# Another written order for the engines' work, fewer filler matmuls and another assignment of tiles to buffers

## The chip, the cores and the metric

The kernel runs on one core of one Trainium2 chip. The core has five engines with instruction sequences of their own: TensorE (PE: matrix products; PEld is its weight load), VectorE (DVE), ScalarE (ACT), GpSimd (POOL), and SyncE (SP), which here issues DMA transfers. Each engine takes its instructions in order. The metric is the device time of one execution in microseconds; several runs are taken, and their median and range are given.

## The reference

```python
# attention: B=4, H=8, S=768, D=64; inputs n_global (8) and n_local (96)
scores = q @ k.transpose(0, 1, 3, 2) / sqrt(D)
keep   = is_global | is_local        # the first 8 keys, and 0 <= i - j < 96
scores = scores - slope[head] * dist # dist: |i - j|, or 96 for a global key that isn't local
a      = softmax(where(keep, scores, -1e9))
x      = (a @ v), heads side by side # 3072 tokens x 512
# feed-forward
h   = x @ w_in                       # 512 -> 2048
g   = where(h >= 1, h, where(h <= -1, 0, (h + 1)**2 / 4))
out = g @ w_out                      # 2048 -> 512
```

The weights arrive as 64-bit floats, q and k as 32-bit floats in blocks of 128 tokens with the head dimension on the partitions.

## The kernel before

The 3072 tokens are 24 units of 128 tokens, numbered 0 to 23: first the four first blocks of the batches (units 0 to 3), then the other five blocks of each batch. Attention is done unit by unit, in two halves of four heads (hf 0 and 1). Two units make a chunk of 256 tokens; the feed-forward part runs over 12 chunks, 0 to 11. Numbers are held as pairs of 16-bit floats, a high part and the rest (names in h and l), so a product takes three matmuls.

**Units 0 to 3** use 32-bit data: first_load (L612) fetches k, q and v, first_scores (L620) makes the scores, masked (L632) adds the bias and takes the minimum on VectorE, expo (L644) the exponential on ScalarE, first_turn (L668) and first_pt (L675) transpose, first_av (L686), scale_x (L694) and first_xt finish the half unit. **Units 4 to 23**: fetch loads a block, conv_hi (L749, ScalarE) and conv_lo (L759 on VectorE for v, L764 and L765 on GpSimd for k and q) split it into halves, conv_check (L773) takes a square sum on ScalarE for a check of the numbers' size. keep_glob (L781, L784) saves the first 32 keys or values of the batch, and set_glob (L792, L794) puts them into a later block. Then scores (L810), masked, expo, split_p (L824 on ScalarE, L826 on VectorE), a transposing DMA, attend (L851), scale_x, split_x and another transposing DMA.

**Weights** come in 32 pieces (0 to 15 of w_in, 16 to 31 of w_out): w_load (L518) is a load of 512 KB on SyncE's queue, w_bits (L532, L536, L540) makes 32-bit floats of the 64-bit ones on VectorE, w_hi (L553, ScalarE), w_scale (L560) and w_lo (L567, GpSimd) split them.

**Feed-forward.** ffn1 (L936) multiplies a chunk by two weight pieces into an h tile; gelu works on it in steps (L955 on ScalarE, L959 and L961 on VectorE, then L969 to L985 on GpSimd and ScalarE) and writes ga and gb tiles. Chunks 0 to 2 multiply these plainly by w_out: ffn2 (L995). Chunks 3 to 11 use a scheme with fewer products: first_products and last_products (L1039) use differences of the weights that diff (L1008 to L1030) prepares once, and fold (L1090, L1093) puts the parts together. put_out stores the result on SyncE's queue.

limits (L429, L431) spreads the two input numbers over the partitions with a small matmul. filler is one 128x512 matmul of zeros (L494) into a tile called spare that nobody reads.

**The order.** Each step is a call that is put into a list called plan, sorted by a planned time. It isn't issued in that order: the list PLACE holds the numbers of the plan's entries, and the calls are made in its order. Each engine's sequence is so the part of PLACE that concerns this engine. An assertion, after(), makes sure that a step that needs another's result stands behind it. Entries 89 to 288 are the 200 fillers; PLACE need not name them all, and 69 are named before.

**The buffers.** Tiles have tags ("ga", "z", "s", ...), and each tag has a fixed number of buffers, two to thirteen. SLOTS says which of them the n-th tile of the tag takes. A tile's first writer waits until all users of the tile that held the buffer before are done.

```python
n = taken[tag] = taken.get(tag, -1) + 1
return p.tile(shape, dtype, tag=f"{tag}_{SLOTS[tag][n]}", bufs=1, name=name)
...
for n in PLACE or range(len(plan)):
    t, _, f, args = plan[n]
    f(*args)
```

Of the kernel before, what the change touches and what calls it, by code (L numbers as in the profile page):

```python
# [26 lines left out]
GLOB = 32  # L27
# [5 lines left out]
SV = 256.0  # L33
# [5 lines left out]
SQK = 128.0  # L39
# [19 lines left out]
HE = {"k": "p", "q": "p", "v": "v"}  # L59
# [282 lines left out]
def fast_path(ctx, tc, q, k, v, nraw, nval, w_in, w_out, out, half, one, stat, marks, badi):  # L342
# [392 lines left out]


    fetched, kblk, kglob, vblk, vglob, qblk = ({} for _ in range(6))

    def fetch(u, kind, j):
        b, i = UNITS[u]  # L740
        r = tl(ins, [P, DM], F32, "in", INS, f"{kind}r{u}_{j}")
# [738 lines left out]
```

## Time and profile before

| | |
|---|---|
| median of the runs | 602.26 us (601.92 to 602.86, 3 runs) |
| the profiled execution | 603.65 us; its span, from the first to the last instruction, 601.8 us |
| granted clock of TensorE, mean | 0.997 of full speed |
| busy over the span | TensorE 580.5 us (96%), GpSimd 500.2 (83%), VectorE 477.7 (79%), ScalarE 441.5 (73%) |
| DMA | 88.19 MB, mean 147 GB/s |

The profile is of one execution, which took a little longer than the runs that were timed. Busy shares are means over the whole span; the stages differ, and the stretch up to about 200 us, in which the first units, the weights and the first chunks are worked on, looks different from what follows.

### The profile page before, as it was taken

Reading aid. Unit: us, or ns where it says so; the run is one execution under the profiler, and the core shown is the slowest. Engines: PE = TensorE matmul, PEld = TensorE weight load, DVE = VectorE, ACT = ScalarE, POOL = GpSimd, SP = SyncE. Lnnn points to the kernel's source line nnn. Section 1 sums busy time; section 2 is a strip of 40 time slices with the busy share of each in tenths; the row PEclk is TensorE's granted clock in tenths of the full one; section 3 lists DMA queues with packets and bytes.
Section 4 is the critical chain, followed back from the end, with each engine's and each line's share of the span. In section 5 each row is a group of like instructions: output and inputs, shape, how many; then the busy total and the mean of one; then the engine's idle time right before and its main releaser. Section 6 shows DMA issues by size and latency. Waiting matters only on the chain.

```text
span 601.8 us, 16582 instructions
## 1 busy us (share of the span) xinstructions
PE 580.5 (96%) x6275; PEld 478.8 (80%) x6275; DVE 477.7 (79%) x1175; ACT 441.5 (73%) x1146; POOL 500.2 (83%) x570
## 2 busy tenths in 40 slices
PE   8999998799999999999999999999999999999995
PEld 4777764356777688888888889888888888898884
DVE  6999999889987667888888888879989878883331
ACT  4998997889866778858787778768768768634330
POOL 5368996695999998899998998899898799579880
PEclk9999999899999999999999999999999999999999
DMA  7647678479660266467598468388487576250011
GB/s 245 207 153 233 203 247 258 102 148 171 123 141 12 62 153 164 119 156 203 131 179 202 125 153 205 104 213 203 120 204 158 153 180 154 77 124 1 2 36 41
DMA packets 144236, 88.19 MB, mean 147 GB/s; under 512 B 108180, under 2 KB 124820, under 8 KB 144148
## 3 DMA queue, kind: packets, MB, share of 16 engines
q1 hardware_dynamic: 144144, 87.05, 57.4%
q8 instruction: 51, 0.84, 0.6%
q14 instruction: 37, 0.30, 0.2%
q10 hardware_dynamic: 4, 0.00, 0.0%
HBM read 54.53 MB, written 6.29 MB: 101 GB/s over the span
## 4 chain that ended last, share of the span: by engine, by line
PE 75%; POOL 9%; DVE 7%; ACT 4%; issue 2%; DMA 2%; POOLq 0%; DVEq 0%; ACTq 0%
PE h L936 31%; PE o L1039 28%; PE o L995 5%; PE av L851 4%; PE s L810 4%; POOL ga L969 2%; DMA wd<-in_moe_w_in_dram 2%; PE spare L494 1%; DVE wd L540 1%; POOL wd L1030 1%; DVE w_bits L532 1%; DVE u L961 1%; POOL kh L765 1%; ACT z L644 1%; DVE w_bits L536 1%
## 5 line engine op out<-in xcount | busy, mean ns | idle before, releaser
L936 PE MATMUL h<-xt,wih 128*128 128x256 f16 x1536 | 255.7, 273 | 3.4 <-DVE u L961 3.4
L936 PE MATMUL h<-xt,wil 128*128 128x256 f16 x768 | 209.4, 273 | 0.0
L936 PEld LDWEIGHTS <-wih 128*128 128x128 f16 x1536 | 148.7, 98 | 27.1 <-DVE u L961 7.7
L644 ACT ACTIVATE z<-z,stat 128x256 f32<-128x256 f32 (+1 forms) x192 | 91.5, 479 | 14.6 <-DVE stat L632 14.6
L980 POOL TENSOR_TENSOR ga<-u,ga 128x512 f16<-128x512 f32 x72 | 89.8, 1249 | 11.2 <-ACT ga L978 10.8
L959 DVE SCALAR_TENSOR_TENSOR h<-h,u 128x512 f32<-128x512 f32 x96 | 66.3, 692 | 38.9 <-ACT u L955 38.4
L1039 PEld LDWEIGHTS <-ga 128*128 128x128 f16 x864 | 83.2, 98 | 10.1
L955 ACT ACTIVATE u<-h,half 128x512 f32<-128x512 f32 x96 | 65.0, 677 | 27.2 <-PE h L936 14.4
L936 PEld LDWEIGHTS <-wil 128*128 128x128 f16 x768 | 75.1, 98 | 8.7
L971 POOL TENSOR_TENSOR u<-u 128x256 f32<-128x256 f32 x72 | 59.9, 835 | 20.0 <-DVE u L961 19.0
L985 POOL TENSOR_TENSOR gb<-u,gb 128x384 f16<-128x384 f32 x72 | 70.2, 978 | 3.5 <-ACT gb L983 3.5
L1039 PE MATMUL o<-wd,ga 128*128 128x256 f16 x432 | 70.7, 273 | 0.0
L1039 PE MATMUL o<-woh,ga 128*128 128x256 f16 x288 | 70.7, 273 | 0.0
L1039 PEld LDWEIGHTS <-gb 128*128 128x128 f16 x648 | 62.4, 98 | 8.0 <-issue 0.6
L978 ACT ACTIVATE ga<-u 128x512 f16<-128x512 f32 x72 | 44.2, 621 | 32.9 <-POOL u L973 30.4
L961 DVE SCALAR_TENSOR_TENSOR u<-u,h 128x512 f32<-128x512 f32 x96 | 65.1, 679 | 3.3 <-POOL kg L781 0.5
L826 DVE SCALAR_TENSOR_TENSOR ph<-z,ph 128x1024 f16<-128x1024 f32 x40 | 56.8, 1423 | 13.0 <-ACT ph L824 13.0
L995 PE MATMUL o<-woh,ga 128*128 128x512 f16 x192 | 61.7, 384 | 1.4 <-ACT woh L553 0.8
L632 DVE CUSTOM_DVE_ANT_0 z<-s,bias 128x256 f32<-128x256 f32 x160 | 58.3, 414 | 5.7 <-PE s L810 5.5
L1039 PE MATMUL o<-wd,gb 128*128 128x256 f16 x432 | 60.4, 273 | 0.6 <-DVE ob L1090 0.6
L995 PEld LDWEIGHTS <-ga 128*128 128x128 f16 x288 | 27.7, 99 | 37.6 <-issue 9.4
L599 DVE TENSOR_REDUCE stat<-c_raw 128x1 f32<-128x256 f32 x128 | 47.9, 405 | 0.0
(132 smaller groups left out, 1185.3 us busy)
## 6 DMA issues: line engine op xcount, KB each, us to landing
wd<-in_moe_w_in_dram SPq DMA_DIRECT2D x16, 512.0 KB, 4.8
wd<-in_moe_w_out_dram SPq DMA_DIRECT2D x16, 512.0 KB, 4.4
c_raw<-in_moe_w_in_dram SPq DMA_DIRECT2D x32, 256.0 KB, 3.0
c_raw<-in_moe_w_out_dram SPq DMA_DIRECT2D x32, 256.0 KB, 3.3
kr<-in_k_dram SPq DMA_DIRECT2D x28, 256.0 KB, 4.1
vr<-in_v_dram SPq DMA_DIRECT2D x28, 256.0 KB, 3.2
qr<-in_q_dram SPq DMA_DIRECT2D x24, 256.0 KB, 4.3
out_dram<-ob SPq DMA_DIRECT2D x23, 256.0 KB, 2.7
```

Of the source, the lines that this page charges most:

```text
L632: nc.vector.tensor_tensor_reduce(out=p32[u, hf][:, hh, :], in0=pts[u, hf][hh // 2][:, hh % 2, 0:n], in1=(own_bias if n == P else bias)[:, ...
L644: nc.scalar.activation(z, z, AF.Exp, bias=nm[:, c : c + 1], scale=-1.0, accum_out=sums[:, c : c + 1])
L826: nc.vector.scalar_tensor_tensor(phs[u, hf][:, 1, :], zf, SP_, phs[u, hf][:, 0, :], op0=ALU.mult, op1=ALU.subtract)
L936: nc.tensor.matmul(hp[:, :, e, :], w[:, dc, f], xt[:, hf, 2 * a + j, :], start=(n == 0), stop=(n == 3 * NDC - 1),)
L955: nc.scalar.activation(u, h, AF.Relu, bias=half, scale=2.0 / (SV * SW), accum_out=su[:, col : col + 1])
L959: nc.vector.scalar_tensor_tensor(h, h, 4.0 / (SV * SW), u, op0=ALU.mult, op1=ALU.max)
L961: nc.vector.scalar_tensor_tensor(u, u, 4.0, h, op0=ALU.min, op1=ALU.mult)
L971: nc.gpsimd.tensor_sub(f[:, 3:7:3], f[:, 0:6:5], f[:, 4:5].to_broadcast([P, 2, P]))
L980: nc.gpsimd.tensor_sub(gas[c, g][:, 1], f[:, 0:4], gas[c, g][:, 0])
L985: nc.gpsimd.tensor_sub(gbs[c, g][:, 1, 0:3], f[:, 4:7], gbs[c, g][:, 0, 0:3])
L995: nc.tensor.matmul(po, a, w[:, f, :], start=(f == 0 and n == 0), stop=(f == NFC - 1 and n == 2))
L1039: nc.tensor.matmul(acc[:, e], x, w, start=first and n == 0, stop=last and n == 2)
```

## The change

Three things. The list PLACE is another permutation of the same entries, without the 32 fillers 126 to 157, so that 37 fillers remain. The digits of SLOTS are others, for all tags; "kg" (the saved global keys) uses one buffer where it used two. And an empty tuple VPU is added, with a function he() that would let some units' v be converted on GpSimd: with VPU empty, conv_lo, conv_check and keep_glob issue what they issued before.

```diff
 PLACE = [
-    1, 2, 0, 13, 41, 4, 28, 20, 10, 3, 46, 89, 90, 91, 92, 93, 5, 8, 6, 11, 7, 51, 19, 94, 95, 96, 97, 98, 99, 100,
-    21, 18, 56, 16, 31, 17, 64, 38, 34, 43, 39, 14, 69, 30, 15, 37, 29, 47, 9, 74, 26, 22, 33, 12, 24, 25, 88, 23, 32,
...
+    0, 2, 1, 10, 13, 8, 20, 11, 4, 29, 3, 5, 6, 7, 89, 90, 91, 31, 15, 21, 16, 19, 18, 14, 38, 30, 39, 43, 34, 41, 26,
+    47, 25, 9, 37, 17, 92, 93, 94, 45, 12, 36, 33, 23, 22, 32, 58, 61, 24, 55, 27, 49, 95, 96, 97, 68, 40, 54, 35, 67,
+    62, 65, 48, 66, 42, 44, 75, 57, 98, 52, 79, 83, 59, 87, 85, 28, 77, 71, 81, 301, 63, 84, 60, 73, 289, 304, 292,
...
 ]
 SLOTS = {
...
-    "k": [int(n, 16) for n in "012012012012102102102102"],
-    "kg": [int(n, 16) for n in "0101"],
-    "o": [int(n, 16) for n in "101010100101010101010101010101010101101010101"],
...
+    "k": [int(n, 16) for n in "201201021020120120120120"],
+    "kg": [int(n, 16) for n in "0000"],
+    "o": [int(n, 16) for n in "101001101010101001100101101001010110010110101"],
...
+VPU = ()
...
+    def he(kind, u):
+        return "p" if kind == "v" and u in VPU else HE[kind]
...
-        if HE[kind] == "v":
+        if he(kind, u) == "v":
...
-            nc.vector.tensor_copy(vglob[b], vblk[b, 0][0:GLOB])
+            (nc.gpsimd if u in VPU else nc.vector).tensor_copy(vglob[b], vblk[b, 0][0:GLOB])
```

The numbers in words, for four stretches of the list on which the prediction rests (each engine's own sequence, only the steps that count there; "fillers 5" is five of them in a row, the numbers of a step are unit and half, weight piece, or pair of pieces and step):

```
TensorE, start    before: positions, fillers 5, limits, fillers 7, first_scores 0.0 and 0.1, fillers 16, first_scores 1.0
                  after:  positions, limits, fillers 3, first_scores 0.1 and 0.0, fillers 3, first_scores 1.0
SyncE, start      before: q0, k0, q1, weight 2, v1, v0, k1, weights 0 and 1, q2, k2, weight 3
                  after:  k0, q0, k1, q1, weight 0, v0, weight 1, k2, q2, weights 2 and 3, v1
ScalarE, piece 31 before: conv_check 6, split_p 4.0, w_hi 31, expo, w_scale 31
                  after:  expo, split_p 4.0, w_hi 31, w_scale 31
VectorE, unit 7   before: set_glob 8, norm 6.0, conv_lo 7, diff 2.0, norm 6.1, diff 2.2, split_p 7.0
                  after:  diff 2.0, diff 2.2, norm 6.1, conv_lo 7, masked 7, split_p 7.0, diff 3.0
```

## Rows read from the trace of the kernel before

**Rows 1.** Busy us (and instructions) of each engine by stretch, granted clock, DMA share, GB/s.
```profile
0.00:50.00 50.00, 45.79 (x334) 32.67 (x334) 42.95 (x160) 39.72 (x124) 26.56 (x32) 1.00 0.62 201
50.00:117.00 67.00, 60.08 (x491) 41.06 (x492) 62.66 (x121) 58.97 (x132) 57.77 (x55) 0.99 0.65 206
117.00:200.00 83.00, 79.21 (x847) 55.30 (x847) 69.34 (x150) 63.45 (x161) 73.59 (x69) 0.98 0.64 130
200.00:588.00 388.00, 387.41 (x4539) 342.78 (x4534) 300.42 (x742) 279.40 (x731) 342.29 (x416) 1.00 0.57 137
```

**Rows 2.** Groups by line: the fillers (busy us, mean ns | idle before).
```profile
L494 PE MATMUL spare<-zeros 128*128 128x512 f16 x69 | 19.8, 409 | 0.0
```

**Rows 3.** Chain that ended last, 117 to 200 us: start us, us, what.
```profile
140.00 1.49 PE s L810 x48
...
144.55 0.58 DVE vh L759
145.13 0.61 DVE d L1008
...
146.27 1.65 POOL df L1023
...
186.58 2.79 PE h L936 x24
```

**Rows 4.** Timeline, TensorE at the start: start us, us, what.
```profile
2.91 2.31 PE L494 MATMUL spare<-zeros 128*128 128x512 f16 x5
...
9.05 3.63 PE L494 MATMUL spare<-zeros 128*128 128x512 f16 x16
12.61 0.71 PE L620 MATMUL s<-kr,qr 64*128 64x128 f32 x8
```

**Rows 5.** Timeline, VectorE; in brackets the idle time before and its releaser.
```profile
5.78 0.16 DVE L431 COPY nval<-pps_n 128x2 f32<-128x2 f32 x1 [0.38 <-PE pps_n L429]
...
9.16 0.29 DVE L632 CUSTOM_DVE_ANT_0 z<-s,wd 128x128 f32<-128x128 f32 x1 [0.92 <-PE s L620]
...
13.35 0.29 DVE L632 CUSTOM_DVE_ANT_0 z<-s,wd 128x128 f32<-128x128 f32 x1 [1.64 <-PE s L620]
...
21.31 0.70 DVE L532 TENSOR_SCALAR spare<-wd 128x512 int32<-128x512 int32 x1 [0.70 <-DMA wd<-in_moe_w_in_dram]
...
75.74 0.70 DVE L959 SCALAR_TENSOR_TENSOR h<-h,u 128x512 f32<-128x512 f32 x1 [1.01 <-ACT u L955]
...
112.71 1.22 DVE L826 SCALAR_TENSOR_TENSOR ph<-z,ph 128x1024 f16<-128x1024 f32 x1 [1.12 <-ACT ph L824]
```

**Rows 6.** Timeline, SyncE's DMA queue at the start.
```profile
2.12 0.43 SPq L518 DMA_DIRECT2D wd<-in_moe_w_in_dram  x1
...
3.62 0.43 SPq L612 DMA_DIRECT2D kr<-in_k_dram  x1
```

**Rows 7.** Timeline around the last weight piece.
```profile
109.86 0.69 DVE L540 SCALAR_TENSOR_TENSOR wd<-wd,w_bits 128x512 int32<-128x512 int32 x1
...
112.58 0.61 ACT L553 ACTIVATE woh<-wd 128x512 f16<-128x512 f32 x1
...
115.50 0.38 PE L995 MATMUL o<-wol,ga 128*128 128x512 f16 x1 [1.87 <-POOL wol L567]
...
115.71 0.59 PE L995 MATMUL o<-woh,ga 128*128 128x512 f16 x2
...
118.45 1.06 PE L995 MATMUL o<-woh,ga 128*128 128x512 f16 x2
```

**Rows 8.** Timeline of two places in the dense part.
```profile
380.11 0.52 ACT L983 ACTIVATE gb<-u 128x384 f16<-128x384 f32 x1 [0.90 <-POOL u L975]
...
381.37 0.49 PE L1039 MATMUL o<-wd,gb 128*128 128x256 f16 x3
...
416.43 1.37 POOL L980 TENSOR_TENSOR ga<-u,ga 128x512 f16<-128x512 f32 x1 [0.20 <-ACT ga L978]
...
417.69 0.49 PE L1039 MATMUL o<-wd,ga 128*128 128x256 f16 x3
```

More of the change, by code (lines that the diff above doesn't have):

```diff
@@ L107 @@
 PLACE = [
[159 rows of a table removed]
[158 rows of a table added]
 ]
 SLOTS = {
-    "ga": [int(n, 16) for n in "0123456789abc012589bc3467a012589bc3467058b360a129c475b809c57836a124b0958614057c3a2b98615a3b61407c2985ab10c95b364728a105b67215c9348a0b725930a261c48b75901247b03ac65891243"],
-    "h": [int(n, 16) for n in "01010101011010101010101010101010101010110010110010101010010101010101010101101010101010101010110011010101010"],
-    "in": [int(n, 16) for n in "01234501254301425304123542015320410231542310542013204532012531402351403251402351"],
-    "k": [int(n, 16) for n in "012012012012102102102102"],
@@ L273 @@
-    "kg": [int(n, 16) for n in "0101"],
-    "o": [int(n, 16) for n in "101010100101010101010101010101010101101010101"],
-    "ob": [int(n, 16) for n in "01220120102101201201201201201021"],
-    "ph": [int(n, 16) for n in "01010101010110101010101010101010101010101010"],
-    "pt": [int(n, 16) for n in "010101010101010110101010101010101010101010100101"],
-    "q": [int(n, 16) for n in "01010101100101010101"],
-    "r": [int(n, 16) for n in "010110101001010110010101010101101001010101011001"],
-    "raw": [int(n, 16) for n in "0101010101010101011010101001010100110010101101011010101100101011"],
@@ L281 @@
-    "s": [int(n, 16) for n in "0123310210301232323032103103210312032130213021302130213021302031021032121301230123012301320123023102312031203120132013023102132031203101320132103203120321032130213021302130213012302130"],
-    "u": [int(n, 16) for n in "01201021022102102102101200120121012021021021021012021021021021021021021021021021021021021021002021021021"],
-    "v": [int(n, 16) for n in "012012001201201202102102"],
-    "x": [int(n, 16) for n in "010101010101011010100101010101010110101010100110"],
@@ L285 @@
-    "xh": [int(n, 16) for n in "0110011001010101010101010101011010101010"],
-    "xt": [int(n, 16) for n in "010101010101"],
-    "z": [int(n, 16) for n in "010101010101001010101101001010101010101010101"],
+    "ga": [int(n, 16) for n in "b469a7318025bc4943c798b07251a839bc460ab7130259cb6a5704b6b1873a590642c8304bc7531a29b0652852b7a34c01698564a086b27c456a935b91745082ac7b62b3b715c62a8b490c3498132b6a0749c640"],
+    "h": [int(n, 16) for n in "11011010111010101010101010010101010101001101110101010010010101010110101010010110101010101010110100101010100"],
@@ new lines @@
+    "in": [int(n, 16) for n in "13520432105435124013454021350215423105314352141054212541013012134231524535142052"],
+    "k": [int(n, 16) for n in "201201021020120120120120"],
+    "kg": [int(n, 16) for n in "0000"],
+    "o": [int(n, 16) for n in "101001101010101001100101101001010110010110101"],
+    "ob": [int(n, 16) for n in "02102202001010021202010121100110"],
+    "ph": [int(n, 16) for n in "00011010101001010110101010100101010101011010"],
+    "pt": [int(n, 16) for n in "010110111010100101100101010110011001011001100110"],
@@ new lines @@
+    "q": [int(n, 16) for n in "01010110100101010110"],
+    "r": [int(n, 16) for n in "011010100110110111011001011010100110100101010101"],
+    "raw": [int(n, 16) for n in "1001100110100110101011000110100011010010101100011010010011010100"],
+    "s": [int(n, 16) for n in "0231213102031232131203120313120301233321330103101210120103212301303210331210320213312010201312231003012300102320321001012323213003321001031222012323230112021313210302123031302113021322"],
+    "u": [int(n, 16) for n in "21212012011201211202102100210202120102102011021020102102102102101201202120120120120102102021002021021021"],
@@ L288 @@
+    "v": [int(n, 16) for n in "012100201201212010201201"],
+    "x": [int(n, 16) for n in "101001010110100110111001101011000110011010010110"],
+    "xh": [int(n, 16) for n in "1010100101100110010101011010100110101001"],
+    "xt": [int(n, 16) for n in "011010101010"],
+    "z": [int(n, 16) for n in "101010101011010101001011001011001100101101001"],
 }
@@ L757, in conv_lo @@
         did.add(("lo", kind, b, j))
-        if HE[kind] == "v":
+        if he(kind, u) == "v":
             nc.vector.scalar_tensor_tensor(f[:, 1, :], r, scale, f[:, 0, :], op0=ALU.mult, op1=ALU.subtract)
             return
-        if HE[kind] == "a":
+        if he(kind, u) == "a":
             nc.scalar.activation(r, r, AF.Copy, scale=scale)
@@ L771, in conv_check @@
         col = {"v": 0, "k": NU, "q": 2 * NU - B}[kind] + (u if kind == "q" else b * NB + j)
-        scale = 1.0 if HE[kind] != "v" else SV if kind == "v" else SQK
+        scale = 1.0 if he(kind, u) != "v" else SV if kind == "v" else SQK
         nc.scalar.activation(r, r, AF.Square, scale=scale, accum_out=sq[:, col : col + 1])
```

312 rows, old and new, of the table PLACE are left out of this document.

## Prediction

> **What bounds the kernel now.** I read the busy time by stage first. From 200 to 588 us TensorE is busy 387.41 of 388 us [rows 1]; behind that only the last products, the folds and the stores are left. I laid the old and the new list side by side, engine by engine: the last entry that changes place on any engine runs just before 280 us of this trace, and from there on, the last chunk and the stores included, all five sequences are the same. So the dense 388 us can only move as a block, and a gain has to come from the first 200 us. There TensorE is busy 45.79, 60.08 and 79.21 us of 50, 67 and 83 [rows 1], and 19.8 us of that are the 69 filler matmuls, which compute nothing [rows 2]. Real work is 165.3 us; 34.7 us of the 200 are idle or filler. That is the reservoir, and no more than a part of it can be had, since TensorE is not what those 200 us wait for.
>
> VectorE is. It is busy 42.95 of the first 50 us and 62.66 of the next 67 [rows 1]: 105.6 of 117 us, so 11.4 us are all that better order can take from it up to the last weight piece. Then GpSimd, busy 73.59 of the 83 us from 117 to 200 [rows 1]. The chain of waits shows how one hands over to the other: scores of unit 7 on TensorE at 140.00, softmax and weight differences on VectorE to 146.2, and from 146.27 GpSimd, through diff, gelu and conversion pieces, until TensorE takes over for good at 186.58 [rows 3]. What I have to forecast is how much earlier VectorE reaches that difference at 145.13; GpSimd's work behind it, and TensorE's, come in the same amount.
>
> **The change part by part.** The empty VPU, the new he() and the choice in keep_glob issue the same instructions as before: nothing. No operation is added but for the order; 32 of the 69 fillers go (numbers 126 to 157). At 19.8 us for 69 [rows 2] they hold 9.2 us of TensorE, of which I count nothing by itself: where TensorE waits, a filler less is a wait more.
>
> *Start, VectorE.* Five fillers stand ahead of the matmul that spreads the limits, and VectorE waits 0.38 us for it; sixteen stand between unit 0's scores and unit 1's, from 9.05 to 12.68, and unit 1's scores start at 12.61 without any wait for data [rows 4]. VectorE waits 0.92 us for the first scores and 1.64 for unit 1's [rows 5]. The new order has the limits matmul with no filler ahead, three fillers before the first scores and three before unit 1's. The loads agree: now unit 1's k is issued at 3.62, behind a weight piece of 512 KB issued at 2.12 [rows 6]; in the new order k and q of units 0 and 1 are the first four loads. The three waits sum to 2.94 us. All of it is the upper bound; the lower is 0.4, if the first scores wait for their load as long as now and only the limits gain. Nearest to the row of the sixteen fillers, I take 2.5.
>
> *Weight loads.* VectorE waits 0.70 us at 21.31 for a weight piece [rows 5], whose buffer is freed by its own earlier step, so the load moves with it. Bounds 0 and 0.7, and I take 0.5. Against it: the fourth weight load now stands ahead of unit 1's v on SyncE's queue and holds it until piece 0 has been unpacked; v is wanted two steps later, and I count nothing.
>
> *ScalarE's stalls.* At 75.74 VectorE waits 1.01 us for ScalarE [rows 5], which sits behind a square sum that waits for GpSimd. The new order moves these square sums (conv_check) back by up to 21 places, seven of them past the weight steps. Bounds 0 and 1.0; I take 0.5.
>
> *Last weight piece.* The work that stands ahead of it on VectorE is 0.2 us more than now, by summing the durations of both orders; that is a loss. Now VectorE ends piece 31 at 110.55 and ScalarE only starts on it at 112.58, with one exponential between its two steps [rows 7]. In the new order the square sum of unit 6 is gone from before it and the two steps stand together: up to 2.0 us for TensorE, which waits for this piece until 115.50 [rows 7]. For VectorE what counts is the 1.12 us wait at 112.71 for ScalarE's split of unit 4 [rows 5], which now would have ended by then. Bounds 0 and 1.1; I take 0.8.
>
> *Unit 7 and the differences.* Scores of unit 7 stand three second-product blocks earlier on TensorE, and on VectorE the step at 145.13 and the one after it stand ahead of the conversion of v7 (0.58, from 144.55 to 145.13 [rows 3]) and of one masked step (0.29 at 9.16 [rows 5]), 0.87 together. Bounds 0, if the step then waits for scores instead, and 0.9; I take 0.8, since the scores end well before it.
>
> *Waits that the new buffers add.* I paired each tile with the tile that held its buffer before, in both orders, and compared the end of the old tile's last use with the first write of the new one, at the times of this trace. Now no pair overlaps. In the new list 37 of 1011 pairs do, 19 of them in the first 200 us. So there 19 writers have to come later or their forerunners earlier than now. Two of them can't cost anything on the chain (a 4-column reciprocal written long before it is used, an output copy with 14 us to spare). For the rest I take a loss of 1.2 us; bounds 0 and 3.5, the second the largest ones on VectorE, ScalarE and GpSimd at full size.
>
> The kg buffers shrink from two to one, and the copies into it lie 14 us or more after the last reader: nothing. Past 280 us the order is the same and TensorE never waits now, so there is nothing to gain there.
>
> Sum: 2.5 + 0.5 + 0.5 - 0.2 + 0.8 + 0.8 - 1.2 = 3.7 us. The profiled execution took 603.65 us with a span of 601.8, so 1.85 lie around the span; it would take 599.95. The median of the runs shown is 602.26, 1.39 below the profiled one; I take the 3.7 off it: **598.6 us**. With every lower bound and the full new waits the sum is -3.3 (slower), with every upper bound 6.4.
>
> **A rule that speaks against it.** The stretch 117 to 200 has a granted clock of 0.98 [rows 1]: after the gaps before 117 two 128x512 matmuls take 1.06 us, against 0.59 for two at 115.71 [rows 7], so the engine sits at 1.2 GHz instead of 2.4 for a while once it has been idle. Fewer fillers mean more idle in the first 45 us. The Trainium skill, page "TensorE: Matmul & The Clock Gate", section on the HAM clock gate, says that the throttled clock is the default and that activity releases it. By that, the fillers bought full clock for the first units; the trace agrees as far as its single fall, behind the gaps before 117. What it would cost is a rival below.
>
> **The rivals.**
> *Clock (0.12).* If TensorE stays at 1.2 GHz until the weights come in quantity, the pieces between VectorE's steps double: unit 1's scores took 0.71 us [rows 4], and each of the 8 half units has some four such pieces, so about 2.8 us each, mostly beside VectorE's weight work. If a third of it (one us per half unit, and half of these units on the chain) shows, 4 us go: about 602.4, no change. For it: the fillers fall from 31 to 12 before 24 us. Against: TensorE still runs most of that stretch, and it has 6.9 us of idle time from 50 to 117 in which to catch up [rows 1].
>
> *Buffers in the dense part (slower, 0.14).* The new list reuses the thirteen "ga" buffers closely. One example: ScalarE writes a gb tile at 380.11, and in the new list that buffer's reader is the products that end at 381.86 [rows 8], so ScalarE, and all behind it, stands 1.75 us. TensorE's cover is thin in places: GpSimd ends a gelu piece at 417.80 and the product that reads it is issued at 417.69, no cover at all [rows 8]. If waits of 1.7 us reach four of them not made up by GpSimd's idle time, 5 to 7 us are lost and the kernel ends near 604. It decides from 3.7 us in sum. Against: only 12 of the 37 overlaps lie past 300 us, 12 us in all, and GpSimd is busy 342.29 of 388 us [rows 1], some 12% free to catch up.
>
> *More than I count (0.17).* If VectorE loses nearly all of its waits and the new buffers cost nothing, 6 us: 596.3.
>
> *Nothing comes through (0.09).* VectorE leads, but GpSimd starts no earlier on the differences at 146.27 [rows 3], since conversions that were pushed back fill its gap: within 1 us of now.
>
> **How the numbers follow.** My own case has 0.48: 596.8 to 600.4. A measurement of this kernel tells 0.2%, 1.2 us, from no change. Faster: mine, the larger gain and half of the clock's chance, 0.71. Same: the rest of the clock's, less 0.01, and the case where nothing comes through, 0.14. Slower: 0.15, the dense part and that 0.01. The range reaches from 595.0 (the larger gain with 1 us more) to 603.2 (past no change, with a third of the slower case).
>
> **What would show it.** Right: unit 1's scores by about 10 us; VectorE without waits of over 0.5 us for TensorE before 20; the last weight piece near 112; GpSimd's diff near 142.5; TensorE dense from about 183 to 584. Wrong: a granted clock under 1 between 10 and 45, TensorE waits after 200, or ScalarE waiting for TensorE at gb tiles with a stall behind.

## The result, and the profile after

| | before | after |
|---|---|---|
| median of the runs | 602.28 us (601.92 to 602.86, 4 runs) | 592.98 us (590.63 to 595.94, 4 runs) |
| profiled execution, span | 603.65, 601.8 us | 592.99, 591.1 us |

The ratio is 0.9847 (95% interval 0.9802 to 0.9892): 9.3 us faster, where 3.7 were forecast, and below the low end of the range, 595.0. Run again beside two of the experiments, the new kernel took 594.70 us (0.9853, 0.9828 to 0.9877). Ratios here and below leave disturbed executions out (one of 1531.62 us of the kernel with the new start and the old rest, two of 603.50 and 604.27 us of the new list without fillers), so where times scatter they differ a little from the ratio of the medians.

The busy time by stage after, with the columns of [rows 1]:

```profile
0.00:50.00 50.00, 44.28 (x351) 34.83 (x352) 45.71 (x168) 42.09 (x129) 30.67 (x36) 1.00 0.79 253
50.00:117.00 67.00, 61.32 (x519) 39.80 (x517) 63.55 (x129) 61.33 (x146) 61.05 (x58) 1.00 0.65 192
117.00:200.00 83.00, 81.60 (x872) 58.08 (x871) 67.22 (x154) 66.69 (x168) 77.27 (x75) 1.00 0.51 108
200.00:588.00 388.00, 384.46 (x4507) 343.02 (x4505) 297.06 (x727) 270.12 (x705) 333.17 (x404) 1.00 0.59 138
```

TensorE's own busy time in the first 200 us is about what it was, but more of it is real: the fillers fell from 19.8 us [rows 2] to 10.9. VectorE is busy 45.71 of 50 us, 2.8 more than before. The granted clock is 1.00 in every stretch; the fall behind the gaps before 117 us [rows 7] is gone.

The group of the fillers, and TensorE's start:

```profile
L494 PE MATMUL spare<-zeros 128*128 128x512 f16 x37 | 10.9, 400 | 0.0
```

```profile
4.90 1.46 PE L494 MATMUL spare<-zeros 128*128 128x512 f16 x3
...
6.29 1.92 PE L620 MATMUL s<-kr,qr 64*128 64x128 f32 x16
8.15 0.82 PE L494 MATMUL spare<-zeros 128*128 128x512 f16 x3
8.90 0.71 PE L620 MATMUL s<-kr,qr 64*128 64x128 f32 x8
...
10.94 1.09 PE L668 MATMUL tp<-ident,z 128*128 128x128 f32 x8
```

Unit 1's scores start at 8.90 instead of 12.61 [rows 4]. The last weight piece, which answers to [rows 7]:

```profile
103.39 0.68 DVE L540 SCALAR_TENSOR_TENSOR wd<-wd,w_bits 128x512 int32<-128x512 int32 x1
...
105.31 0.61 ACT L553 ACTIVATE woh<-wd 128x512 f16<-128x512 f32 x1
...
106.66 1.15 POOL L567 TENSOR_TENSOR wol<-wd,woh 128x512 f16<-128x512 f32 x1 [1.36 <-ACT wd L560]
...
107.86 0.38 PE L998 MATMUL o<-wol,ga 128*128 128x512 f16 x1 [0.59 <-POOL wol L567]
```

VectorE ends the piece at 104.07, 6.5 us earlier, and TensorE waits 0.59 us where it waited 1.87.

Where the lead arises is read best from the start of the same steps in both traces. For VectorE I split it in three: the change of its idle time up to the step, the change in busy time of instructions that stand ahead of the step in both lists, and the work that the new list puts behind it or ahead of it.

| VectorE's step | before, us | after | lead | idle | same instructions shorter | work moved |
|---|---|---|---|---|---|---|
| unit 1, a masked step | 14.97 | 9.73 | 5.24 | 2.34 | 1.28 | 1.62 |
| unit 1, last step | 29.00 | 22.34 | 6.66 | 3.77 | 1.56 | 1.34 |
| piece 31, last step | 109.86 | 103.39 | 6.48 | 2.95 | 3.72 | -0.20 |
| first step of the third difference (145.04 before) | 145.04 | 133.13 | 11.91 | 6.23 | 4.61 | 1.07 |

TensorE is 11.3 us ahead at its first product of chunk 3 (220.90 before), and 10.7 at its last instruction. So the lead comes in two places, 6.7 us in the first 29 and another 5 between 104 and 133; the dense part gives back 0.6. The 10.7 us are more than the 9.3 of the medians because the traced execution of the kernel before was 1.4 us longer than its median. And 4.6 of the 11.9 us are neither waiting nor order: VectorE's same instructions were done in less time.

That last number is not the new order's alone. A second trace of the new kernel (an execution of 595.30 us) leads by 5.9, 6.3 and 10.7 us at the last three steps of the table, and at the third difference 6.5 of this are idle time, 1.2 moved work and only 3.1 shorter instructions. And three kernels of the experiments that keep VectorE's old order and only leave fillers out have 1.5 to 2.0 us of shorter instructions at the same step. What holds in both traces is the idle time.

How the shorter instructions look in the rows: the start of VectorE and of GpSimd, first before, then after.

```profile
4.60 1.07 POOL L457 TENSOR_SCALAR bias<-bias 128x256 f32<-128x256 f32 x1
...
4.64 0.43 DVE L439 TENSOR_SCALAR m_own<-m_own 128x128 f32<-128x128 f32 x1
...
5.75 0.72 POOL L459 TENSOR_TENSOR bias<-bias 128x256 f32<-128x256 f32 x1
...
5.97 0.59 DVE L445 TENSOR_SCALAR m_own<-bias,nval 128x128 f32<-128x128 f32 x1
```

```profile
4.56 0.23 DVE L439 TENSOR_SCALAR m_own<-m_own 128x128 f32<-128x128 f32 x1
...
5.22 0.29 DVE L445 TENSOR_SCALAR m_own<-bias,nval 128x128 f32<-128x128 f32 x1
...
7.57 0.29 DVE L632 CUSTOM_DVE_ANT_0 z<-s,wd 128x128 f32<-128x128 f32 x1 [0.49 <-PE s L620]
...
15.50 1.16 POOL L567 TENSOR_TENSOR wil<-wd,wih 128x512 f16<-128x512 f32 x1 [14.65 <-ACT wd L560]
```

Beside GpSimd's mask steps the two took 0.43 and 0.59 us, alone 0.23 and 0.29. In the new list GpSimd idles until 15.50. Later it shows in the mean of a group: the x split on VectorE took 755 ns before and 662 after, the v conversion 1023 and 915 (first before, then after; mean ns of one behind the bar). In the second trace of the new kernel the two means are 712 and 931.

```profile
L867 DVE TENSOR_TENSOR xh<-x,xh 128x256 f16<-128x256 f32 x40 | 29.5, 755 | 3.2 <-ACT xh L865 3.2
L759 DVE SCALAR_TENSOR_TENSOR vh<-vr,vh 128x512 f16<-128x512 f32 x24 | 24.4, 1023 | 0.8 <-ACT vh L749 0.8
```

```profile
L870 DVE TENSOR_TENSOR xh<-x,xh 128x256 f16<-128x256 f32 x40 | 25.9, 662 | 4.1 <-ACT xh L868 4.0
L762 DVE SCALAR_TENSOR_TENSOR vh<-vr,vh 128x512 f16<-128x512 f32 x24 | 21.8, 915 | 0.7 <-ACT vh L752 0.7
```

### The profile page after: what moved, and what is told of

The parts are those of the page before. It is cut to its first block, busy times and chain, and to the rows that moved or that the text cites. A ratio compares the mean times of both kernels' runs of the same rounds, so it can differ in the third digit from the quotient of the medians.

```text
span 591.1 us, 16452 instructions
## 1 busy us (share of the span) xinstructions
PE 571.7 (97%) x6243; PEld 475.7 (80%) x6243; DVE 473.5 (80%) x1175; ACT 440.2 (74%) x1146; POOL 502.2 (85%) x570
## 4 chain that ended last, share of the span: by engine, by line
PE 66%; DVE 11%; ACT 10%; DMA 5%; POOL 4%; issue 3%; ACTq 0%; SPq 0%; DVEq 0%; POOLq 0%
PE h L939 30%; PE o L1042 26%; ACT z L644 5%; PE s L813 4%; PE av L854 4%; PE o L998 3%; DMA wd<-in_moe_w_out_dram 2%; DMA wd<-in_moe_w_in_dram 2%; DVE wd L540 2%; DVE u L964 1%; DVE h L962 1%; ACT ph L827 1%; POOL ga L972 1%; DVE w_bits L536 1%; DVE ph L829 1%
## 5 line engine op out<-in xcount | busy, mean ns | idle before, releaser
L983 POOL TENSOR_TENSOR ga<-u,ga 128x512 f16<-128x512 f32 x72 | 88.3, 1227 | 10.1 <-ACT ga L981 9.8
L988 POOL TENSOR_TENSOR gb<-u,gb 128x384 f16<-128x384 f32 x72 | 72.0, 1002 | 3.7 <-ACT gb L986 3.7
```

Source lines behind the costliest of these rows:

```text
L983: nc.gpsimd.tensor_sub(gas[c, g][:, 1], f[:, 0:4], gas[c, g][:, 0])
L988: nc.gpsimd.tensor_sub(gbs[c, g][:, 1, 0:3], f[:, 4:7], gbs[c, g][:, 0, 0:3])
```

## The experiments

OLD and NEW stand for the two lists, written here as operations on them. Line numbers in the rows move by up to three between kernels. "Buffers by the old rule" are chosen so: of the buffers of the tag that are free in the written order, the one whose last use ended first; for OLD this gives back nearly all of the old pairing. A list that is put together of both can keep neither kernel's buffers, so those versions have SLOTS of their own too. Leads are against before at the same step: "VectorE at 29 us" is unit 1's last step.

**All fillers out of the old list.**

```diff
+PLACE = [n for n in OLD if not 89 <= n <= 288]
```

> The old list and buffers, with all 69 fillers taken out (they compute nothing). Theory A (the fillers hold TensorE, so what they occupy is the gain): 8 to 18 us less than before. Theory B (TensorE waits where it had a filler; only the start, where VectorE waits for the scores behind them, gains): 2 to 3 us less. Theory C (without fillers TensorE stays at 1.2 GHz for the first units): no change or slower, and a granted clock under 1 before 45 us.

604.02 against 603.02 us, ratio 1.0012 (0.9992 to 1.0032): nothing. VectorE led by 2.4 us at 29 us, 2.2 were left at the end of the profiled execution, and the timed runs scattered from 601.41 to 606.05. Theory A falls. The clock did suffer: it is full only from 13.8 us (7.07 before), and falls again between 30 and 40:

```profile
30.00:40.00 10.00, 8.46 (x61) 6.74 (x59) 8.97 (x24) 9.10 (x28) 5.95 (x6) 0.83 0.51 161
```

**Only the fillers at the start thinned, in two ways.**

```diff
+PLACE = [n for n in OLD if n not in (*range(89, 98), *range(101, 114))]   # 22 out
+PLACE = [n for n in OLD if n not in range(101, 114)]                      # 13 out
```

> The old list and buffers, with 22 of the 28 fillers ahead of unit 1's scores taken out (5 ahead of the limits, 4 ahead of unit 0's scores, 13 ahead of unit 1's), as few there as in the new list. If the start was mis-sized because of the fillers alone: 4 to 6 us less than before, as VectorE is 5 us earlier at unit 1 in the new kernel. If the order of the loads and of GpSimd's mask steps counts as much: 1.5 to 3 us less.

> The old list with its 12 fillers ahead of unit 0's scores kept, and 13 of the 16 ahead of unit 1's taken out. In the run with 22 of the 28 taken out full clock came only at 14.3 us (7.07 before), and VectorE won 1.5 us by 29 us. If the late clock ate the rest there: full clock by 8 us here, VectorE 2 to 3 us earlier at 29 us, and 599 to 601. If the old start is held by its loads and by what stands ahead of unit 1 on VectorE: 1.5 us as there, 601 to 602.

0.9970 (0.9957 to 0.9984) and 0.9976 (0.9962 to 0.9989), about 1.5 us each, and VectorE 1.5 us ahead at 29 us in both. They pay in different ways. Eight transposes of unit 0 in the first and in the second kernel:

```profile
12.20 1.91 PE L669 MATMUL tp<-ident,z 128*128 128x128 f32 x8
```

```profile
12.89 1.04 PE L669 MATMUL tp<-ident,z 128*128 128x128 f32 x8
```

With 22 out, TensorE is still at 1.2 GHz at 12.2 us, and VectorE waits 0.61, 0.48 and 1.07 us for the first three scores. With 13 out it is at full clock, and VectorE waits 1.31 us for the first scores, behind the 12 fillers that are left. Neither gets much more than 1.5 us out of the old order.

**The start new and the rest old, and the other way round.**

```diff
+PLACE = NEW[:155] + [n for n in OLD if n not in NEW[:155]]   # and SLOTS by the old rule
+PLACE = OLD[:204] + [n for n in NEW if n not in OLD[:204]]   # the same, "ob" held 3 us longer
```

> The new list up to the end of unit 1 (its first 155 entries), then the rest in the old order with its fillers, buffers by the old rule. Theory A (the start gives most of the gain and the rest keeps it): 5 to 6.5 us less than before, 596 to 597. Theory B (the sum of the prediction for start and weight loads): 3 us less. Theory C (the old order of what follows gives the lead back, since it waits for GpSimd at 146 us): within 1 us of before.

> The counterpart: the old list up to the end of unit 1 (its first 204 entries), then the rest in the new order, buffers by the old rule with output buffers held 3 us longer, for the store. If the start's lead (VectorE 6.7 us ahead at 29 us) is what the new kernel lives on: 597 to 601. If the order of the rest makes the gain whatever the start: 592 to 595.

1.0019 (1.0008 to 1.0030), and 0.9987 (0.9969 to 1.0004). The first has all of the start's lead, 6.3 us at 29 us, but 1.4 at piece 8 (40.27 before). VectorE loses it to ScalarE, in rows of its timeline:

```profile
25.47 0.18 DVE L657 RECIPROCAL r<-stat 128x4 f32<-128x4 f32 x1 [1.28 <-ACT z L645]
...
33.90 0.42 DVE L720 TENSOR_TENSOR xt<-xtp,xt 128x256 f16<-128x256 f32 x1 [1.36 <-ACT xt L718]
```

With 0.79 us at 30.08 these are 3.4 us, and 1.3 us of work that the new list had moved back comes due at the seam. TensorE's scores of unit 7 (139.93 before) still come 2.1 us earlier, but VectorE and GpSimd lead by only 0.7 at the third difference, and behind a step of the next one that waits for an output buffer GpSimd is 0.9 late:

```profile
148.91 1.15 POOL L1017 TENSOR_TENSOR dt<-woh,wol 128x512 f32<-128x512 f16 x1 [1.74 <-DMA out_dram<-ob]
```

The counterpart has no lead at 29 us, 1.2 at piece 31 and 4.0 at the third difference, and 2.3 are left at the end of its profiled execution. So the rest by itself makes about 4 us up to 141 us, and the start 6.3; neither keeps them alone. That wait for a store comes from the old rule for buffers (the next experiment), so the end of the first version is not a matter of the order alone; most of its lead was gone before.

**The new list with the old buffer rule, then with new output buffers alone.**

```diff
+SLOTS = old_rule(NEW)
+SLOTS = old_rule(NEW) | {"ob": SLOTS_NEW["ob"]}
```

> The new list, with buffers chosen by the rule that reproduces nearly all of the old assignment (of the buffers that are free in the written order, the one whose last use ended first), two buffers for the saved keys. If the new assignment costs what the prediction took (1.2 us): 1 to 3 us less than the new kernel, 590 to 592. If the buffers bind nowhere: as the new kernel, 593. If the new assignment earns part of the 9.3 us: over 595.

> As the run of the new list with the old buffer rule, but the output buffers (tag ob, which the weight differences dt share with the outputs) as in the new list. There GpSimd waited 2.31 us at 114.00 with dt1 for the store of chunk 0's output; in the new kernel dt1 takes the buffer of dt0 and doesn't wait. If this one wait is what the old rule costs: as the new kernel, 590 to 595, 1.3 to 1.8% less than before. If the other tags' buffers cost as much: 596 to 597, as with the old rule throughout.

0.9905 (0.9879 to 0.9931), 596.69 us, and 0.9803 (0.9770 to 0.9836), 592.04. The new buffers don't cost the 1.2 us that I took; it is the old rule that costs, some 3.5 us against the new kernel (0.9905 less 0.9847, of 602) or 3.1 against its second measurement (0.9853), and all of it is in one tag. (The interval overlaps the first measurement's by a little, not the second's.) GpSimd's second dt in the old rule and in the kernel with new output buffers:

```profile
114.00 1.16 POOL L1017 TENSOR_TENSOR dt<-woh,wol 128x512 f32<-128x512 f16 x1 [2.31 <-DMA out_dram<-ob]
```

```profile
111.90 1.16 POOL L1017 TENSOR_TENSOR dt<-woh,wol 128x512 f32<-128x512 f16 x1
```

An output tile's last user is the store, not the engine that filled it. dt1 took such a tile's buffer and stood 2.31 us, with the q and k conversions behind it; VectorE's third difference then came 2.7 us later.

**The old fillers in the new list, no fillers in it, and its first nine.**

```diff
+PLACE = fillers of OLD ahead of the same TensorE steps, the rest as NEW
+PLACE = [n for n in NEW if not 89 <= n <= 288]
+PLACE = [n for n in NEW if not 98 <= n <= 288]
```

> The new list and its buffers, but with the 69 fillers of the old list, each ahead of the TensorE step that it preceded there (5 ahead of the limits, 7 ahead of unit 0's scores, 16 ahead of unit 1's). If fillers hold TensorE wherever they stand: the 9 us that 32 of them occupy come back, 600 to 602. If only those of the start hold VectorE up: 1.5 to 3 us more than the new kernel, 594 to 597. If they cost nothing: 593.

> The new list and buffers with its 37 fillers taken out too. If the fillers that are left still hold TensorE: 2 to 5 us less than the new kernel, 588 to 591. If TensorE waits in their place: 592 to 594. If it falls to 1.2 GHz without them, as the old list without fillers did from 30 to 40 us (granted clock 0.83 there): a granted clock under 1 before 70 us, and 594 to 598.

> The new list and buffers with the first nine of its fillers (those ahead of the first scores and of unit 1's) and without the 28 later ones, from 13 us on. Without any fillers TensorE's pieces took twice as long until 32.8 us (four transposes 0.85 us instead of 0.44), and VectorE lost its whole lead. If the nine are what brings TensorE to full clock: transposes at full speed from 10 us on, VectorE's lead at 29 us 6 us or more, and 590 to 595 as the new kernel, less if the 28 held TensorE. If the later ones are needed to keep the clock: half clock between 15 and 60 us and 596 to 602.

1.0011 (0.9986 to 1.0035), 603.64 us: with 69 fillers the whole gain is gone, and in the first 30 us already. VectorE's waits there:

```profile
10.40 0.29 DVE L634 CUSTOM_DVE_ANT_0 z<-s,wd 128x128 f32<-128x128 f32 x1 [1.82 <-PE s L622]
...
14.61 0.29 DVE L634 CUSTOM_DVE_ANT_0 z<-s,wd 128x128 f32<-128x128 f32 x1 [2.65 <-PE s L622]
```

VectorE is 7.6 us later than in the new kernel at unit 1's last step, 7.2 of them idle. But without any filler most of the gain is gone too: 601.17 us (594.47 to 604.27), ratio 0.9943 (0.9911 to 0.9975). Its TensorE and VectorE in the first 33 us, in an execution of 603.50 us, one of its longest:

```profile
11.33 1.97 PE L667 MATMUL tp<-ident,z 128*128 128x128 f32 x8
...
30.57 0.63 PE L938 MATMUL h<-xt,wih 128*128 128x256 f16 x2
...
32.96 0.38 PE L938 MATMUL h<-xt,wih 128*128 128x256 f16 x2
```

```profile
18.94 0.42 DVE L693 SCALAR_TENSOR_TENSOR x<-av,r 128x256 f32<-128x256 f32 x1 [1.11 <-PE av L685]
...
26.83 0.29 DVE L631 CUSTOM_DVE_ANT_0 z<-s,wd 128x128 f32<-128x128 f32 x1 [1.09 <-PE s L619]
```

Eight transposes take 1.97 us where they took 1.09 in the new kernel, and the first ffn1 goes from 0.63 to 0.38 us a pair only at 32.8: TensorE works at 1.2 GHz until then. VectorE's lead, 5.4 us at 14.97, is 0.6 at 29 us. Whether the clock rose earlier in the executions of 594 to 598 us no trace shows. The first nine fillers are enough: 594.96 us, 0.9891 (0.9855 to 0.9927), beside 594.70 for the new kernel, with a lead of 6.4 us at 29 us, though the granted clock falls to 0.83 between 40 and 50 us. The 28 later ones buy nothing that can be measured.

**GpSimd's mask steps back at the start.**

```diff
+PLACE = NEW with the nine far steps behind distances, clip, slope and masked steps as in OLD
```

> The new list and its buffers, but GpSimd's nine steps of the far mask stand where the old list has them, beside VectorE's first 10 us, where the new list leaves GpSimd idle. If VectorE's own steps take longer while GpSimd works (0.22 against 0.54 us for a copy of saved keys in the trace of before): VectorE's masked step of unit 1 comes 1.0 to 1.5 us later than in the new kernel, and the end 0.5 to 1.5 us later. If durations don't depend on GpSimd: no change at either place, or earlier, since GpSimd has less to do later.

The place: VectorE's first steps stretch again.

```profile
4.64 0.43 DVE L440 TENSOR_SCALAR m_own<-m_own 128x128 f32<-128x128 f32 x1
...
5.75 0.72 POOL L460 TENSOR_TENSOR bias<-bias 128x256 f32<-128x256 f32 x1
...
5.83 0.80 DVE L447 SCALAR_TENSOR_TENSOR m_own<-m_own,nval 128x128 f32<-128x128 f32 x1
```

0.80 us beside GpSimd, 0.35 for the same line in the new kernel. Up to unit 1's masked step the same instructions take 0.98 us more, 0.45 of idle time cover a part, and the step comes 0.53 us later. The end shows nothing: 594.20 us (592.28 to 595.83), 0.9856. So the price of overlapping is real at the place, and at the start too small for the end. This trace says more: with VectorE's instructions only 2.0 us shorter than before at the third difference, its lead there is 13.1 us, and 10.0 of that are idle time. The new order can make the lead without the shorter instructions.

**The new list up to the last weight piece, then the old one.**

```diff
+PLACE = NEW[:634] + [n for n in OLD if n not in NEW[:634]]   # and SLOTS of its own
```

> The new list up to the last weight piece (its first 634 entries), then the rest in the old order; output buffers chosen so that no step waits for a store if another is free. If the lead at the last weight piece (6.5 us) goes through the old rest: 595.5 to 597. If the new order of what follows brings the other 4 us and the old one can't use the lead: 599 to 602. If the rest's order counts for nothing: 593.

> The new kernel itself, beside the other two: 591 to 595, 1.3 to 1.8% less than before.

599.58 us, 0.9939 (0.9920 to 0.9958), beside 594.70 for the new kernel, which came as expected. VectorE led by 8.7 us at piece 31, and by 4.2 at the third difference, 4.1 at the end. Between them (VectorE, TensorE, and the stretch 70 to 117):

```profile
109.81 0.18 DVE L657 RECIPROCAL r<-stat 128x4 f32<-128x4 f32 x1 [3.13 <-ACT z L645]
...
120.56 0.42 DVE L633 CUSTOM_DVE_ANT_0 z<-s,bias 128x256 f32<-128x256 f32 x1 [2.71 <-PE s L814]
```

```profile
111.75 0.59 PE L999 MATMUL o<-woh,ga 128*128 128x512 f16 x1 [4.24 <-ACT ob L1116]
```

```profile
70.00:117.00 47.00, 39.66 (x296) 22.62 (x296) 39.58 (x90) 41.19 (x103) 37.93 (x37) 0.93 0.66 193
```

ScalarE is late with the exponentials and with chunk 0's output, TensorE idles 4.24 us and falls to 1.2 GHz (granted clock 0.93 over the stretch). A part of this is the seam, since the square sums that the new list had pushed back come due there; I did not separate that.

## Why the prediction was wrong

The direction and the place (the first 200 us, VectorE's lead handed on to the dense block) were right, the size was 2.5 times too small. By its own steps:

- **Start and weight loads.** The sum took 2.5 and 0.5 us, with 2.94 and 0.7 as upper bounds, because these were VectorE's waits. It gained 6.7. The waits were sized well enough: idle time fell by 3.8 us, a little more than both bounds together (3.1 in the second trace). What had no term was the rest of it: 1.6 us by which the same instructions were shorter, and 1.3 us of weight and norm steps that stand behind and are paid by piece 31.
- **The fillers.** Their 9.2 us were counted as nothing by themselves. That holds in the old order (all out: 1.0012) and not in the new, where having the old 69 back costs 9.9 us (1.0011 less 0.9847, of 602). A filler costs what the engine behind it could have used. The rival on the clock had the mechanism right: without any filler TensorE stays at 1.2 GHz until 32.8 us. I gave it 0.12 for this kernel, where nine fillers before 11 us are enough. The rule of the Trainium skill, page "TensorE: Matmul & The Clock Gate", section on the HAM clock gate, that the throttled clock is the default, agrees with the traces here: the first fillers take 0.46 us [rows 4] or 0.49 (three in 1.46 at 4.90), those after 8 us 0.23 to 0.27.
- **ScalarE's stalls and the last weight piece.** The terms 0.5, 0.8 and -0.2 make 1.1. The lead went from 6.66 to 6.48 between 29 us and piece 31, and 0.8 of the idle time won by then was lost again (3.77 to 2.95), so nothing of the first came; behind the piece the lead grew.
- **From the last weight piece to the differences.** The sum took 0.8 for one wait, 0.8 for unit 7 and a loss of 1.2; from piece 31 to the third difference VectorE gained 5.4 us (11.91 less 6.48): 3.3 of waits, 0.9 of shorter instructions, 1.3 of order. Here the list of waits was short. Beside the 1.12 us at 112.71 [rows 5] VectorE waited twice more in the trace of before, for ScalarE's split of unit 5 and for the scores of unit 6, and the prediction gives neither a term:

```profile
121.94 1.28 DVE L826 SCALAR_TENSOR_TENSOR ph<-z,ph 128x1024 f16<-128x1024 f32 x1 [0.94 <-ACT ph L824]
...
124.80 0.42 DVE L632 CUSTOM_DVE_ANT_0 z<-s,bias 128x256 f32<-128x256 f32 x1 [1.58 <-PE s L810]
```

In the new kernel VectorE waits 0.41 us there in two pieces before its third difference, 0.39 in the second trace. The old start with the new rest gains 2.8 us on this stretch by itself (3.99 less 1.16).
- **Waits for the new buffers.** The sum took a loss of 1.2 us, by pairing the new list at the old times. At the new times no wait for a store is left on GpSimd (ScalarE has one of 1.1 us, at 227.66), and against the new list under the old rule the new buffers gain 3.1 to 3.5 us. The dense-part rival did not come: 0.6 us given back after 220 us, 1.5 in the second trace.
- **What would show it.** Unit 1's scores by about 10 us (8.90) and no wait over 0.5 for TensorE (0.49) came true. The last piece near 112, the difference near 142.5 and the end near 584 were all too late: 107.86, 135.93 and 576.7.

So three steps of the sum failed. At the third difference the sum had 4.3 us of waits, 0.6 of order and a loss of 1.2, 3.7 in all, and VectorE led by 11.9. First, the waits listed were taken for all that there are, and new ones were added for the buffers: idle time fell by 6.2 us. Second, VectorE's instructions were taken to last as long as before: they lasted 4.6 us less (3.1 in the second trace, and not all of it the order's doing). Third, the order was worth 1.1 instead of 0.6. The direction came by the path that was forecast, so it is no luck.

The case "more than I count", 596.3, was the nearest, and it too counted waits alone. Not settled is how much each of the two later pieces (order and shorter instructions) is worth at the end: the halves of the list don't add up in time (1.0019 and 0.9987 against 0.9847), since each seam brings waits of its own. No version tried beats the new kernel clearly; the one with old buffers but for ob (0.9803) overlaps it.

## What to carry to other kernels

When an order is laid anew, don't bound the gain by the few waits that you can name: sum the idle time of the engine up to each step that matters, and split the lead at a step into idle time, work moved, and the busy time of the same instructions. Look for instructions whose duration depends on what runs beside them, and take a second trace of the same kernel to see how much of that is the order's. A lead gained early is kept only if each engine behind it can use it, so test the halves of an order, and look in their traces for the engine that gives it back. Count the store as the last user of an output buffer before another engine's tile is put into it.

## What was not expected of the hardware

VectorE's instructions between SBUF tiles can stretch while GpSimd works: 0.23 to 0.43 us, 0.29 to 0.59, and 0.35 to 0.80 in the rows above. Those that read the scores from PSUM don't change, 0.29 us beside GpSimd (before) and 0.28 to 0.29 alone (after):

```profile
8.59 1.14 POOL L467 TENSOR_SCALAR bias<-bias,nval 128x256 f32<-128x256 f32 x1
...
9.38 0.29 DVE L632 CUSTOM_DVE_ANT_0 z<-s,wd 128x128 f32<-128x128 f32 x1
```

Over the whole trace of before the 40 x splits (L867) take 402 to 1376 ns, the 96 gelu steps on h in PSUM (L959) 680 to 700.

The Trainium skill, page "SBUF — State Buffer", section "SBUF: two separate sides", states that VectorE (in some of its instructions) and GpSimd share a pair of ports under an exclusive lock: who starts first holds it for its whole instruction, and the other blocks. The rows agree only in part: the step of 0.80 us ends 0.16 us after the GpSimd step beside it (5.83 and 5.75), but the one of 0.43 starts 0.04 us after a GpSimd step of 1.07 and ends 0.60 before it.

TensorE worked at 1.2 GHz for a long time nearly without a pause: in the stretch 10 to 20 us of the new list without fillers it was busy 9.82 of 10 us with 32-bit scores, transposes and products at half speed, and it rose in the first ffn1 with 16-bit data. With the new list's fillers it is there by 8.15 us, where three take 0.82. The granted clock in the profile reads 1.00 all the same:

```profile
10.00:20.00 10.00, 9.82 (x50) 8.81 (x50) 7.02 (x33) 6.50 (x26) 3.37 (x3) 1.00 0.52 176
```

Its first record in that trace is at 32.78 us, and what lies before it is shown as full speed. Before a first record only durations tell the clock.
